# The order of an expert's last row groups, and of the second expert's transposes and w2 loads, in an attention + mixture-of-experts kernel

## The chip, the cores and the metric

The kernel runs on one core of one Trainium2 chip. The metric is device time in microseconds (us) of one execution, lower is better. In what follows PE is TensorE (matmuls; PEld its weight loads), DVE is VectorE, ACT is ScalarE, POOL is GpSimd and SP is SyncE, which here issues nearly all plain DMAs and all DMA transposes in one queue. POOL issues the indirect DMAs (gathers and scatters of rows).

## The reference, cut to what matters

Attention over 4 batches of 768 positions and 8 heads of 64 gives `x`, 3072 rows of 512. Then a mixture of experts is computed on `x`:

```python
logits = x @ w_gate
noisy_logits = logits + np.log1p(np.exp(x @ w_noise)) * noise
top2 = np.argpartition(-noisy_logits, 2, axis=1)[:, :2]   # two of eight experts for a row
...
for e in range(E):                                        # 8 experts
    for k in range(2):
        mask = top2[:, k] == e
        h = np.maximum(x[mask] @ w1[e], 0.0)               # 512 -> 1024
        out[mask] += top2_w[mask, k, None] * (h @ w2[e])   # 1024 -> 512
```

All of it is float32. The change touches the loop over the experts alone.

## The kernel before, in words

**Numbers.** TensorE works on float16. Each float32 operand is kept as a high half and a low half (names ending in `h` and `l`, such as `w1h`/`w1l`, `hth`/`htl`), and a product is three passes: high by high, low by high, high by low. ACT makes the high half by a cast, DVE the low half by a subtraction.

**Experts by rank.** The experts are sorted by how many rows chose them. Rank `e` has room for `CAPS[e]` rows: 800, 832, 808, 800, 784, 776, 768, 768. These are six groups of 128 rows (`c` = 0 to 5) and, up to rank 5, a last partial group (`c = LAST = 6`), the **tail**, of 32, 64, 40, 32, 16 and 8 rows. Where the tail has at most 32 rows (`four(e, c)`: ranks 0, 3, 4 and 5) its second matmul is spread over four quarters of the PE array, and DVE must add four quarters up (L920, four instructions) where a full group takes one (L931).

**Rows in.** For a group POOL gathers the rows into `xg` (L90), ACT and DVE make the halves in `x`, and SP issues a DMA transpose into `xte` (ranks 0 and 1: `x_gather`, `x_trans`, lines L812 to L814; later ranks `plan_x`: `xs_gather`, three DVE sums in `xs_sums` L1292 to L1296, `xs_hi` with L1312, `xs_lo` with L1322, transposes at L1328 into `xte`, `xl`, or borrowed parts of `w2h`/`w2l`).

**First matmul.** Ranks 0 and 1 use `mm1` (L854) in two column halves; rank 1's first half needs groups 0 to 2 transposed. From rank 2 on, `seven` computes it as seven products of half-sized blocks instead of eight (L1359). The products 1 and 5 of a rank's first slice form its **head** (`seven_head(n)`); the head reads the tail columns of `x` too. ACT copies their results (L1380, L1383), DVE adds them to later ones (L1385, L1387) and makes `htl` (L1394).

**Second matmul.** For each group, three passes of eight matmuls into one PSUM tile `pt` (two of these in turn): `w2h` by `hth`, `w2l` by `hth`, `w2h` by `htl` (L1431; the tail of quarters L1425; rank 0 L909). Then DVE scales the result and adds the earlier output `prev`, gathered by POOL, and POOL scatters `y` to `out`.

**Weights.** A quarter of w1 or w2 is 512 KB: `w_load` issues it on SP into one of four `stg` buffers, `w_hi` (ACT L740) and `w_lo` (DVE L758) split it. w1 of ranks 2 and later also gets sums (`plan_w1`: L1339, L1348, L1352).

**What sets the order.** Each engine runs its instructions in the order in which the program writes them. For ranks 1 and up, `on(t, f, ...)` files small steps under a number `t`, and `hook(t)` issues them; in the second matmul `hook(32 + 3c)`, `hook(33 + 3c)` and `hook(34 + 3c)` stand behind the first pass, the second pass and the output of group `c`. The groups run 0, 1, ..., 5, then the tail; the next rank's head stands ahead of the tail (or of group 5 where there is no tail). For rank 1 the code is written out: in rank 0's `mm1(0, 1, f)` loop, steps f = 2 to 5 split rank 1's w1 and load its w2, steps 5 to 7 transpose its groups 0 to 2; the loop over rank 0's groups 3 to 6 splits w2 and transposes groups 3 to 6.

Of the kernel before, what the change touches and what calls it, by code (L numbers as in the profile page):

```python
# [25 lines left out]
E, F = 8, 1024  # L26
# [37 lines left out]
def attn_moe(ctx, tc, qt, kt, vt, wgn, noise, w1, w2, out):  # L64
# [660 lines left out]
    def w_load(e, i):  # L725
        s = stage.tile([P, SW], F32, name="stg")[:, :1024]
        SG[e, i] = s
        if i == 0:
            EV[e] = nc.values_load(eid[0:1, e:e + 1], engines=[mybir.EngineType.SP], min_val=0, max_val=E - 1) if e else 0
        if i < 4:  # L730
            nc.sync.dma_start(s, w1.rearrange("e d f -> (e d) f")[bass.ds(EV[e] * DM + i * P, P)])
        else:
            i -= 4
            rows = bass.ds(EV[e] * F + 2 * i * P, 2 * P)
            nc.sync.dma_start(s.rearrange("p (c d) -> p c d", c=2),
                              w2.rearrange("e f d -> (e f) d")[rows].rearrange("(c p) d -> p c d", p=P))
# [51 lines left out]
    def chunks(e):  # L788
        return -(-CAPS[e] // P)
# [644 lines left out]
    for f in range(FC):  # L1434
        mm1(0, 1, f)
        if f < 2:
            gate_tr(f + 4, og)
        if f == 1:
            gate_ur(og)
            decode_rest()  # L1440
            last_ids()
        if 2 <= f < 6:
            w_split(1, f - 2)
            w_load(1, f + 2)
        if f == 5:
            count_over(og)
        if f > 1:
            x_gather(1, f - 2)
        if f > 4:
            x_trans(1, f - 5)  # L1450
    x_gather(1, 6)
    for c in range(3, chunks(0)):
        w_split(1, c + 1)
        x_trans(1, c)
        mm2(0, c, None)
    seven_init()
    G["w2"] = WT[0]
    for e in range(2, E):
# [28 lines left out]

    for e in range(1, E):
        pv = []

        def prev():
            if len(pv) < chunks(e):
                pv.append(prev_gather(e, len(pv)))

        n = e + 1
        if e == 1:
            on(0, tail_ids)
            plan_x(n, 0, 0, (3, 3, 3), (4, 4), (5, 5, 5, 5))
            plan_x(n, 1, 1, (6, 6, 6), (7, 7), (8, 8, 8, 8))
            plan_w1(n, 0, 1, 9, 9, 10, 10, 10)  # L1500
            plan_w1(n, 1, 2, 11, 11, 12, 12, 12)
            plan_x(n, 2, 7, (13, 13, 13), (14, 14), (15, 15, 15, 15))
            plan_w1(n, 2, 11, 33, 33, 34, 34, 34)
            plan_x(n, 3, 12, (35, 35, 35), (36, 36), (37, 37, 37, 37))
            plan_w1(n, 3, 13, 38, 38, 39, 39, 39)
        else:
            for i, (a, b) in enumerate(((3, 4), (4, 7), (8, 14), (15, 21))):
                on(a, w_hi, e, 4 + i)
                on(b, w_lo, e, 4 + i)
            on(36, tail_next, e)  # L1510
            if n < E:
                plan_x(n, 0, None, (9, 11, 12), (10, 13), (15, 16, 18, 19))
                plan_x(n, 1, None, (22, 23, 25), (24, 27), (28, 29, 29, 31))
                plan_w1(n, 0, 8, 32, 32, 33, 33, 34)
                plan_w1(n, 1, 15, 35, 35, 36, 36, 37)
                plan_x(n, 2, 20, (38, 38, 38), (39, 39), (40, 40, 40, 40))
                plan_w1(n, 2, 35, 41, 41, 42, 42, 43)
                plan_x(n, 3, 32, (44, 44, 44), (45, 45), (46, 46, 46, 46))
                plan_w1(n, 3, 38, 47, 47, 48, 48, 49)
            if e > 2:  # L1520
                on(4, w_load, e, 6)
                on(4, w_load, e, 7)
        if n + 1 < E:
            on(40 if e == 1 else 43, xs_gather, n + 1, 0)
            on(42 if e == 1 else 47, xs_gather, n + 1, 1)
        if n < E:
            on(44, w_load, n, 4)
            on(44, w_load, n, 5)
        if e == 1:
            on(48, w_load, n, 6)  # L1530
            on(48, w_load, n, 7)
        for t in (17, 20, 23):
            on(t, prev)
        if e == 1:
            for half in range(2):
                for f in range(FC):
                    mm1(e, half, f)
                    hook(8 * half + f)
            for t in range(16, 32):
                hook(t)  # L1540
        else:
            hi, lo = seven(e, 0, 2)
            hi()
            lo()
            hook(3)
            seven(e, 0, 6)
            for t in range(4, 7):
                hook(t)
            for i in range(1, 5):
                if i < 4:  # L1550
                    seven(e, i, 1)
                    hook(7 * i)
                    seven(e, i, 5)
                    hook(7 * i + 1)
                h7 = seven(e, i - 1, 7)
                h7[0]()
                hook(7 * i + 2 if i < 4 else 28)
                if i < 4:
                    h2 = seven(e, i, 2)
                    h2[0]()  # L1560
                    h7[1]()
                    hook(7 * i + 3)
                    seven(e, i, 6)
                    h2[1]()
                    hook(7 * i + 4)
                else:
                    py = psum.tile([P, 512], F32, name="pt", bufs=2)
                    mm2_part(e, 0, py, 0, range(7), True, False)
                    h7[1]()
                    hook(29)  # L1570
                h3 = seven(e, i - 1, 3)
                h3[0]()
                hook(7 * i + 5 if i < 4 else 30)
                h4 = seven(e, i - 1, 4)
                h4[0]()
                h3[1]()
                h4[1]()
                hook(7 * i + 6 if i < 4 else 31)
        for c in range(chunks(e)):
            if c == chunks(e) - 1 and n < E:  # L1580
                seven_head(n)
            if c or e == 1:
                py = psum.tile([P, 512], F32, name="pt", bufs=2)
                for i, k in enumerate((0, 2, 1)):
                    if e == 1:
                        mm2_pass(e, c, py, k, 1)
                    else:
                        mm2_part(e, c, py, k, range(FC), i == 0, i == 2)
                    if i < 2:
                        hook(32 + 3 * c + i)  # L1590
            else:
                for k in (2, 1):
                    mm2_part(e, 0, py, k, range(7), False, False)
                    hook(33 - k // 2)
                for k in (0, 2, 1):
                    mm2_part(e, 0, py, k, (7,), False, k == 1)
            mm2_out(e, c, py, pv[c])
            prev()
            hook(34 + 3 * c)
        for t in range(60):  # L1600
            hook(t)
# [104 lines left out]
```

## Time and profile before

| | us |
|---|---|
| three runs | 642.48, 644.54, 645.26 (median 644.54) |
| the profiled execution's own time | 642.6 |
| its span, first to last instruction | 640.8 |
| PE busy in the span | 622.5 |
| DVE busy | 481.3 |
| ACT busy | 315.9 |
| POOL busy | 249.0 |

The profiled execution is one run with its own time; the span is 1.8 us shorter. Attention and routing fill about the first 130 us, rank 0 lasts to about 201, rank 1 to about 268, and each later rank takes about 60. A row of the profile gives a line of the kernel, the engine, the operation, what it writes and reads, and its time; in square brackets stands how long the engine was idle before it, and what ended that.

### The profile page before, as it was taken

The page shows a single profiled execution, that of the slowest core. Times are in us where ns is not written, and L with a number is a line of the kernel's source. Part 1 is how long each engine was busy: PE and PEld are TensorE (multiplying, and loading weights), DVE is VectorE, ACT ScalarE, POOL GpSimd, SP SyncE. Part 2 cuts the span into 40 slices and gives each one's busy share as a digit, 9 for nine tenths or more (in the row PEclk, how much of TensorE's full clock was granted, in tenths as well). Part 3 has the DMA queues.
Part 4 walks back from the last instruction along what each step waited for, and adds up shares of the span by engine and source line. Part 5 has one row for each costly group of instructions (what it writes and reads, how often), then busy time and mean ns, then how long its engine had stood idle before and what let it go on. Part 6 is the DMA issues. An engine that isn't in the chain of part 4 may idle for free.

```text
span 640.8 us, 14153 instructions
## 1 busy us (share of the span) xinstructions
PE 622.5 (97%) x5295; PEld 358.8 (56%) x5295; DVE 481.3 (75%) x1039; ACT 315.9 (49%) x692; POOL 249.0 (39%) x432
## 2 busy tenths in 40 slices
PE   8999999999999999999999999999999999999995
PEld 7778777765654544555455544554554455445542
DVE  5768999889796797188868887987898679757410
ACT  4868988941253553075437534654464255425200
POOL 4442224203254324532573266336523532333041
PEclk9999999999999999999999999999999999999998
DMA  9999986788379976547886597759677767763021
GB/s 308 333 292 351 292 266 201 222 318 250 118 217 171 253 186 170 211 122 140 209 265 152 131 228 245 181 133 250 201 189 156 218 205 166 182 198 105 3 96 51
DMA packets 123708, 127.93 MB, mean 200 GB/s; under 512 B 83242, under 2 KB 86674, under 8 KB 123630
## 3 DMA queue, kind: packets, MB, share of 16 engines
q1 hardware_dynamic: 111838, 90.66, 53.3%
q0 software_dynamic: 11792, 36.27, 18.0%
q8 instruction: 44, 0.72, 0.5%
q14 instruction: 34, 0.28, 0.1%
HBM read 81.85 MB, written 25.61 MB: 168 GB/s over the span
## 4 chain that ended last, share of the span: by engine, by line
PE 82%; DVE 6%; issue 3%; DMA 3%; ACT 2%; POOL 1%; SPq 1%; POOLq 0%; DVEq 0%; ACTq 0%
PE pt L1431 29%; PE h L1359 16%; PE h L854 8%; PE pt L909 5%; PE pt L341 3%; PE pt L1359 3%; PE o L1359 3%; PE s L318 3%; PE o L354 3%; PE h L909 2%; DMA xte<-x 2%; PE pt L378 1%; PE o L246 1%; DVE y L920 1%; DVE htl L1394 1%
## 5 line engine op out<-in xcount | busy, mean ns | idle before, releaser
L90 POOL DMA_INDIRECT out_dram<-y,tb x52 | 69.3, 1333 | 169.4 <-DVE y L931 131.6
L90 POOL DMA_INDIRECT xg<-xd,tb x54 | 60.1, 1112 | 118.1 <-DVE dsc L653 32.3
L1431 PEld LDWEIGHTS <-hth 128*128 128x128 f16 x576 | 56.4, 98 | 66.7
L931 DVE SCALAR_TENSOR_TENSOR y<-pt,tb,prev 128x512 f32<-128x512 f32 x42 | 31.5, 750 | 67.4 <-PE pt L1431 49.8
L1359 PEld LDWEIGHTS <-w1h 128*128 128x128 f16 x504 | 48.9, 98 | 38.0 <-issue 4.1
L1431 PE MATMUL pt<-w2h,hth 128*128 128x512 f16 x288 | 69.0, 379 | 0.0
L1431 PE MATMUL pt<-w2h,htl 128*128 128x512 f16 x288 | 69.0, 379 | 0.0
L1431 PE MATMUL pt<-w2l,hth 128*128 128x512 f16 x288 | 69.0, 379 | 0.0
L1359 PEld LDWEIGHTS <-w1l 128*128 128x128 f16 x504 | 49.3, 98 | 34.9
L90 POOL DMA_INDIRECT prev<-out_dram,tb x45 | 52.4, 1165 | 23.7 <-issue 12.8
L333 ACT ACTIVATE p<-s,nm 128x120 f32<-128x120 f32 x192 | 51.0, 376 | 0.8
L854 PE MATMUL h<-xte,w1h 128*128 128x384 f16 (+2 forms) x248 | 48.9, 336 | 1.1 <-DMA xte<-x 1.1
L1431 PEld LDWEIGHTS <-htl 128*128 128x128 f16 x288 | 28.2, 98 | 34.0
L1348 ACT ACTIVATE w1h<-stg 128x768 f16<-128x768 f32 (+1 forms) x24 | 22.7, 944 | 37.9 <-DVE stg L1339 37.9
L1391 ACT ACTIVATE hth<-h 128x384 f16<-128x384 f32 (+4 forms) x48 | 23.8, 496 | 35.6 <-PE h L1359 35.6
L1348 ACT ACTIVATE w1l<-stg 128x768 f16<-128x768 f32 (+1 forms) x24 | 22.5, 942 | 37.2 <-DVE stg L1339 37.2
L1359 PE MATMUL h<-xte,w1h 128*128 128x384 f16 (+4 forms) x180 | 39.7, 329 | 0.7 <-DVE h L1385 0.4
L1359 PE MATMUL h<-xte,w1l 128*128 128x384 f16 (+4 forms) x180 | 39.7, 329 | 0.0
L1339 DVE TENSOR_TENSOR stg<-stg 128x256 f32<-128x256 f32 x96 | 36.2, 419 | 0.8
L854 PEld LDWEIGHTS <-w1h 128*128 128x128 f16 x256 | 24.7, 98 | 20.5 <-issue 2.2
L1312 ACT ACTIVATE x<-xt 128x512 f16<-128x512 f32 (+2 forms) x44 | 26.3, 625 | 19.6 <-issue 17.3
L1394 DVE SCALAR_TENSOR_TENSOR htl<-h,hth 128x384 f16<-128x384 f32 (+4 forms) x48 | 26.3, 562 | 11.8 <-ACT hth L1391 11.5
(301 smaller groups left out, 1292.0 us busy)
## 6 DMA issues: line engine op xcount, KB each, us to landing
stg<-in_w_dram SPq DMA_DIRECT2D x64, 512.0 KB
q<-in_qt_dram SPq DMA_DIRECT2D x24, 256.0 KB
xd<-x SPq DMA_DIRECT2D x24, 256.0 KB
out_dram<-xg SPq DMA_DIRECT2D x8, 768.0 KB
kb<-in_kt_dram SPq DMA_DIRECT2D x6, 768.0 KB
hth<-in_vt_dram SPq DMA_DIRECT2D x12, 260.0 KB
htl<-in_vt_dram SPq DMA_DIRECT2D x16, 195.0 KB
ve<-in_vt_dram SPq DMA_DIRECT2D x12, 260.0 KB
```

The costliest lines, as they stand in the source:

```text
L90: return nc.gpsimd.indirect_dma_start(**kw)
L333: nc.scalar.activation(PE_[t][:, a, hp, :], SC[t][:, a, hp, :], AF.Exp, bias=NM[t][:, 1, a, hp:hp + 1], scale=0.125)
L854: nc.tensor.matmul(ph[:, :n], w1_of(w, wn, c, f), x[:, xo + c, c0:c1], start=(k == 0), stop=(k == 11))
L909: nc.tensor.matmul(py, hx[:, f, c * P:c * P + P], wv[:, f, :], start=st, stop=sp)
L931: nc.vector.scalar_tensor_tensor(y, py[:, :d], gw, pv[:, :d], op0=OP.mult, op1=OP.add)
L1312: nc.scalar.activation(t[:r, c:c + k], src, AF.Copy)
L1339: nc.vector.tensor_tensor(o, x, y, op=op)
L1348: nc.scalar.activation(hi, x, AF.Copy, scale=W1S)
L1359: nc.tensor.matmul(ph[:, :h], w[:, la, a, P * j:P * j + P], x[:, j, :h], start=start and k == 0, stop=k == 5, skip_group_check=True)
L1391: nc.scalar.activation(hh[:, f, t], src, AF.Relu)
L1394: nc.vector.scalar_tensor_tensor(hl[:, f, t], src, 0.0, hh[:, f, t], op0=OP.max, op1=OP.subtract)
L1431: nc.tensor.matmul(py, x, wv[:, f, :], start=st, stop=sp, skip_group_check=True)
```

## The change

The diff does two things.

- **Second rank (e = 1).** In rank 0's last stretch the transposes of rank 1's groups 0 to 3 move into steps f = 4 to 7 of the `mm1` loop, its w2 loads go behind them (two at f = 6 and 7, two in the loop over rank 0's groups), two of the four w1 splits move into that loop, and the w2 splits move behind it; the last three go to the first three hooks of rank 1's own `mm1`. The sums and splits of rank 2's first groups are filed two hooks later. `count_over` goes behind the loop.
- **Tails (ranks 3, 4 and 5).** The tail is computed ahead of group 5 (`early`, `turns`), and the next rank's head is put behind group 5's second pass. The steps of the next rank's tail are filed one hook earlier, those of its last w1 quarter under the new places.

```diff
-        if 2 <= f < 6:
+        if 2 <= f < 4:
             w_split(1, f - 2)
-            w_load(1, f + 2)
-        if f == 5:
-            count_over(og)
+        if f > 3:
+            x_trans(1, f - 4)
         if f > 1:
             x_gather(1, f - 2)
-        if f > 4:
-            x_trans(1, f - 5)
+        if f > 5:
+            w_load(1, f - 2)
     x_gather(1, 6)
+    count_over(og)
     for c in range(3, chunks(0)):
-        w_split(1, c + 1)
-        x_trans(1, c)
+        if c < 5:
+            w_split(1, c - 1)
+            w_load(1, c + 3)
+        if c < 6:
+            x_trans(1, c + 1)
         mm2(0, c, None)
+    w_split(1, 4)
...
+        turns = list(range(chunks(e)))
+        early = e > 1 and chunks(e) > LAST and four(e, LAST)
+        if early:
+            turns[-2:] = turns[:-3:-1]
...
-            plan_x(n, 0, 0, (3, 3, 3), (4, 4), (5, 5, 5, 5))
-            plan_x(n, 1, 1, (6, 6, 6), (7, 7), (8, 8, 8, 8))
+            for t, i in ((0, 5), (1, 6), (2, 7)):
+                on(t, w_split, n - 1, i)
+            plan_x(n, 0, 0, (5, 5, 5), (6, 6), (7, 7, 7, 7))
+            plan_x(n, 1, 1, (8, 8, 8), (9, 9), (10, 10, 10, 10))
...
-                plan_x(n, 3, 32, (44, 44, 44), (45, 45), (46, 46, 46, 46))
-                plan_w1(n, 3, 38, 47, 47, 48, 48, 49)
+                plan_x(n, 3, 32, *(((43, 43, 43), (44, 44), (45,) * 4) if early else ((44, 44, 44), (45, 45), (46,) * 4)))
+                plan_w1(n, 3, 38, *((50, 50, 51, 47, 48) if early else (47, 47, 48, 48, 49)))
...
-        for c in range(chunks(e)):
-            if c == chunks(e) - 1 and n < E:
+        for m, c in enumerate(turns):
+            if c == turns[-1] and n < E and not early:
                 seven_head(n)
...
                     if i < 2:
                         hook(32 + 3 * c + i)
+                    if i == 1 and early and c == turns[-1]:
+                        seven_head(n)
...
-            mm2_out(e, c, py, pv[c])
+            mm2_out(e, c, py, pv[m])
```

**Place 1, SP, rank 0's last stretch.** The queue before: w2 loads of rank 1 (`stg<-in_w2`), then the transposes of its groups.

```order
L735 DMA stg_3536<-in_w2_dram 128x2x512
...
L735 DMA stg_3605<-in_w2_dram 128x2x512
L814 DMA_TRANSPOSE xte_2960<-x_3622 128x8x128
L814 DMA_TRANSPOSE xte_2960<-x_3645 128x8x128
L814 DMA_TRANSPOSE xte_2960<-x_3668 128x8x128
L814 DMA_TRANSPOSE xte_2960<-x_3678 128x8x128
```

The same queue with the change:

```order
L814 DMA_TRANSPOSE xte_2960<-x_3576 128x8x128
L814 DMA_TRANSPOSE xte_2960<-x_3599 128x8x128
L814 DMA_TRANSPOSE xte_2960<-x_3622 128x8x128
...
L735 DMA stg_3630<-in_w2_dram 128x2x512
L814 DMA_TRANSPOSE xte_2960<-x_3647 128x8x128
...
L735 DMA stg_3655<-in_w2_dram 128x2x512
```

Three transposes now stand ahead of the first w2 load, where four loads stood ahead of the first transpose.

**Place 1, ACT, the same stretch.** L860 is rank 0's relu of slice f, L740 the cast of a weight quarter, L812 the cast of a gathered group; before, from the relu of f = 4:

```order
L860 ACTIVATE hth_89<-h_3565 128x416
L740 ACTIVATE w1h1_2956<-stg_3308 128x1024
L860 ACTIVATE hth_89<-h_3588 128x416
L740 ACTIVATE w1h1_2956<-stg_3310 128x1024
L812 ACTIVATE x_3622<-xg0_165 128x512
L860 ACTIVATE hth_89<-h_3626 128x416
L812 ACTIVATE x_3645<-xg0_165 128x512
L860 ACTIVATE hth_89<-h_3649 128x416
```

With the change, from the same relu:

```order
L860 ACTIVATE hth_89<-h_3561 128x416
L812 ACTIVATE x_3576<-xg0_165 128x512
L860 ACTIVATE hth_89<-h_3584 128x416
L812 ACTIVATE x_3599<-xg0_165 128x512
L860 ACTIVATE hth_89<-h_3607 128x416
L812 ACTIVATE x_3622<-xg1_166 128x512
L860 ACTIVATE hth_89<-h_3632 128x416
L812 ACTIVATE x_3647<-xg1_166 128x512
```

Three casts of gathered groups now stand ahead of the last relu (f = 7), where two stood.

**Place 2, SP, the end of rank 3.** The transposes of 16 columns are those of rank 4's tail: two of high halves, then two of low halves (into `xl`). Before:

```order
L735 DMA stg_5750<-in_w2_dram 128x2x512
...
L735 DMA stg_5752<-in_w2_dram 128x2x512
L1328 DMA_TRANSPOSE xte_2629<-x_5762 128x6x16
L1328 DMA_TRANSPOSE xte_2629<-x_5766 128x8x16
L1328 DMA_TRANSPOSE xl_2961<-x_5784 128x6x16
L1328 DMA_TRANSPOSE xl_2961<-x_5788 128x8x16
```

With the change:

```order
L1328 DMA_TRANSPOSE xte_2629<-x_5750 128x6x16
L1328 DMA_TRANSPOSE xte_2629<-x_5754 128x8x16
...
L735 DMA stg_5758<-in_w2_dram 128x2x512
...
L735 DMA stg_5760<-in_w2_dram 128x2x512
L1328 DMA_TRANSPOSE xl_2961<-x_5770 128x6x16
L1328 DMA_TRANSPOSE xl_2961<-x_5774 128x8x16
```

The two w2 loads moved from ahead of the high halves to between the high and the low halves.

**Place 2, DVE, the end of rank 3.** L1322 makes the low halves of rank 4's tail, the L931 of `prev_2964` is the output of group 4, L920 those of the tail. Before:

```order
L931 SCALAR_TENSOR_TENSOR y<-pt,tb,prev_2964 128x512
L1322 TENSOR_TENSOR x<-xg_166,x 16x512
L1322 TENSOR_TENSOR x<-xg_166,x 16x256
L1322 TENSOR_TENSOR x<-xt,x 16x512 x2
L1339 TENSOR_TENSOR stg<-stg 128x256 x4
L1352 SCALAR_TENSOR_TENSOR w1l_2957<-stg,w1l_2957 128x768
L931 SCALAR_TENSOR_TENSOR y<-pt,tb,prev_2965 128x512
L1352 SCALAR_TENSOR_TENSOR w1l_2957<-stg,w1l_2957 128x1024
L920 SCALAR_TENSOR_TENSOR y<-pt,tb,prev_2966 32x512
L920 SCALAR_TENSOR_TENSOR y<-pt,tb,y 32x512 x3
L1394 SCALAR_TENSOR_TENSOR htl<-o,hth 128x392
L1385 TENSOR_TENSOR h<-h,p_5853 128x392
```

With the change:

```order
L1322 TENSOR_TENSOR x<-xg_166,x 16x512
L1322 TENSOR_TENSOR x<-xg_166,x 16x256
L1322 TENSOR_TENSOR x<-xt,x 16x512 x2
L931 SCALAR_TENSOR_TENSOR y<-pt,tb,prev_2964 128x512
L1339 TENSOR_TENSOR stg<-stg 128x256 x4
L920 SCALAR_TENSOR_TENSOR y<-pt,tb,prev_2965 32x512
L920 SCALAR_TENSOR_TENSOR y<-pt,tb,y 32x512 x3
L1352 SCALAR_TENSOR_TENSOR w1l_2957<-stg,w1l_2957 128x768
L1352 SCALAR_TENSOR_TENSOR w1l_2957<-stg,w1l_2957 128x1024
L931 SCALAR_TENSOR_TENSOR y<-pt,tb,prev_2966 128x512
L1394 SCALAR_TENSOR_TENSOR htl<-o,hth 128x392
L1385 TENSOR_TENSOR h<-h,p_5873 128x392
```

The low halves moved ahead of group 4's output, and the tail's four additions moved from just ahead of rank 4's first L1394 and L1385 to ahead of two w1 splits and group 5's output.

## Rows read from the trace of the kernel before

**Rows 1.** The page, busy time: us, share of the span and instructions of each engine.

```profile
PE 622.5 (97%) x5295; PEld 358.8 (56%) x5295; DVE 481.3 (75%) x1039; ACT 315.9 (49%) x692; POOL 249.0 (39%) x432
```

**Rows 2.** Busy time by stretch. The columns are the stretch, its length, then busy us (and instructions) of PE, PEld, DVE, ACT and POOL, the granted clock of PE, the DMA engines' mean busy share, and GB/s.

```profile
200.90:202.10 1.20, 0.11 (x5) 0.08 (x2) 1.20 (x3) 0.00 (x0) 1.20 (x1) 1.00 1.03 211
202.10:633.00 430.90, 429.81 (x2377) 222.40 (x2378) 315.01 (x542) 185.27 (x320) 177.92 (x286) 1.00 0.67 175
394.00:407.00 13.00, 12.71 (x91) 6.86 (x90) 11.17 (x19) 8.49 (x16) 3.45 (x6) 1.00 0.66 198
455.00:468.00 13.00, 12.64 (x92) 6.91 (x90) 11.19 (x19) 8.48 (x17) 4.07 (x6) 1.00 0.66 198
516.00:529.00 13.00, 12.57 (x93) 6.91 (x90) 11.22 (x19) 8.62 (x16) 3.33 (x6) 1.00 0.63 198
```

**Rows 3.** The chain of work that ended last, two pieces ahead of rank 1's first matmul: start, length, what.

```profile
186.74 3.94 DMA xg<-xd,tb
190.68 11.24 DMA xte<-x
```

**Rows 4.** The timeline of SP's queue in that stretch: start, length of the issuing, line, what, count.

```profile
179.39 5.27 SPq L735 DMA_DIRECT2D stg<-in_w_dram  x4
186.61 18.39 SPq L814 DMA_TRANSPOSE xte<-x  x7
```

**Rows 5.** The timeline of the engines in that stretch, cut to the gathers of rank 1's groups 2 and 4 (POOL), the casts of its groups 1, 2, 4 and 5 (ACT L812), rank 0's relu of f = 7 (ACT L860), and the first matmuls of rank 0's groups 3 and 5 and of rank 1 (PE).

```profile
180.56 1.31 POOL L90 DMA_INDIRECT xg<-xd,tb  x1 [0.23 <-issue]
183.85 1.89 PE L909 MATMUL pt<-w2h,hth 128*128 128x512 f16 x8
184.17 0.63 ACT L812 ACTIVATE x<-xg 128x512 f16<-128x512 f32 x1 [1.72 <-DMA xg<-xd,tb]
184.71 0.50 ACT L860 ACTIVATE hth<-h 128x416 f16<-128x416 f32 x1
...
186.73 0.63 ACT L812 ACTIVATE x<-xg 128x512 f16<-128x512 f32 x1 [1.52 <-DMA xg<-xd,tb]
186.74 1.00 POOL L90 DMA_INDIRECT xg<-xd,tb  x1 [3.15 <-DVE x L813]
...
194.21 1.89 PE L909 MATMUL pt<-w2h,hth 128*128 128x512 f16 x8
...
195.55 0.63 ACT L812 ACTIVATE x<-xg 128x512 f16<-128x512 f32 x1 [4.34 <-issue]
...
202.05 0.81 PE L854 MATMUL h<-xte,w1h 128*128 128x384 f16 x4 [1.09 <-DMA xte<-x]
```

**Rows 6.** The timeline of a gather with few other transfers about it, and of the cast that waited for it (rank 0's group 3).

```profile
147.97 1.00 POOL L90 DMA_INDIRECT xg<-xd,tb  x1 [19.83 <-DVE dsc L653]
...
151.99 0.63 ACT L812 ACTIVATE x<-xg 128x512 f16<-128x512 f32 x1 [2.90 <-DMA xg<-xd,tb]
```

**Rows 7.** The groups of instructions by line, the split of a w2 quarter on DVE (count, busy us, mean ns, idle before).

```profile
L758 DVE SCALAR_TENSOR_TENSOR w2l<-stg,w2h 128x1024 f16<-128x1024 f32 x28 | 33.5, 1215 | 0.0
```

**Rows 8.** The busy time of the stretch of rank 1's first matmul, and of the 2.4 us in which the two w2 loads at the end of rank 3 moved, by the columns of rows 2.

```profile
200.00:236.00 36.00, 34.91 (x213) 19.16 (x206) 28.77 (x51) 17.14 (x32) 14.94 (x26) 1.00 0.90 220
384.70:387.10 2.40, 2.40 (x12) 1.07 (x11) 0.76 (x2) 1.98 (x3) 1.96 (x5) 1.00 1.02 351
```

**Rows 9.** The timeline at the end of rank 3, up to the head of rank 4: SP's w2 loads and the transposes of rank 4's tail, ACT's last cast for them, DVE's output of group 4 and low halves, PE's first two passes of group 5 and the head, whose matmuls on `xl` read the low halves.

```profile
381.71 1.17 SPq L735 DMA_DIRECT2D stg<-in_w_dram  x2
383.25 4.05 SPq L1328 DMA_TRANSPOSE xte<-x  x2
...
385.53 0.63 ACT L1312 ACTIVATE x<-xt 16x512 f16<-16x512 f32 x1 [0.21 <-DVE xt L1296]
...
387.11 1.89 PE L1431 MATMUL pt<-w2h,hth 128*128 128x512 f16 x8
387.31 0.75 DVE L931 SCALAR_TENSOR_TENSOR y<-pt,tb,prev 128x512 f32<-128x512 f32 x1 [1.82 <-PE pt L1431]
...
388.84 1.89 PE L1431 MATMUL pt<-w2l,hth 128*128 128x512 f16 x8
...
389.03 2.37 SPq L1328 DMA_TRANSPOSE xl<-x  x2
...
392.29 0.83 PE L1359 MATMUL o<-xte,w1h 128*128 128x392 f16 x4
392.96 0.49 PE L1359 MATMUL o<-xl,w1h 128*128 128x392 f16 x2
...
393.95 0.49 PE L1359 MATMUL h<-xl,w1h 128*128 128x392 f16 x2
```

**Rows 10.** The timeline behind that: rank 3's tail on PE, its four additions on DVE, rank 4's products after its head, and the add (L1385) that one of them waits for.

```profile
394.38 0.61 PE L1425 MATMUL pt<-w2h,hth 128*32 128x512 f16 x8
395.79 0.84 PE L1359 MATMUL o<-xte,w1h 128*128 128x392 f16 x4
395.91 0.74 DVE L920 SCALAR_TENSOR_TENSOR y<-pt,tb,prev 32x512 f32<-32x512 f32 x1 [1.53 <-PE pt L1425]
396.68 2.31 DVE L920 SCALAR_TENSOR_TENSOR y<-pt,tb,y 32x512 f32<-32x512 f32 x3
...
399.50 0.56 DVE L1385 TENSOR_TENSOR h<-h,p 128x392 f32<-128x392 f32 x1
...
400.12 0.82 PE L1359 MATMUL h<-xte,w1h 128*128 128x392 f16 x4 [0.18 <-DVE h L1385]
```

More of the change, by code (lines that the diff above doesn't have):

```diff
@@ L1489, in attn_moe @@
         pv = []
+        turns = list(range(chunks(e)))
+        early = e > 1 and chunks(e) > LAST and four(e, LAST)
+        if early:
+            turns[-2:] = turns[:-3:-1]
         def prev():
             if len(pv) < chunks(e):
-                pv.append(prev_gather(e, len(pv)))
+                pv.append(prev_gather(e, turns[len(pv)]))
         n = e + 1
```

## The prediction

> **What bounds the kernel now.** I read the page first: PE is busy 97% of the span, far above any other engine [rows 1]. So I looked for the stretches in which PE is not busy. From 202.1 to 633 it is busy 429.81 of 430.90 us, and the missing 1.09 us lie in three short stretches, one behind each tail of quarters: 0.29, 0.36 and 0.43 us [rows 2]. Just ahead, between 200.9 and 202.1, it is idle for 1.09 us, ended by the landing of a transpose into `xte` [rows 2, 5]. These are the places that the diff touches, and together they are 2.18 us of 642.6 us, the profiled execution's own time. That is the first thing to see: nothing in the diff removes PE work, so what it can win in the expert loop is bounded by 2.18 us, or 0.34%.
>
> The first wait, read backwards through the chain: rank 1's first matmul waits for a transpose that SP issued at 190.68 and that landed 11.24 us later [rows 3]. SP issued its four w2 loads from 179.39 on and the seven transposes behind them [rows 4]. The other three waits are alike; at the end of rank 3, DVE spends 395.91 to 398.99 on the four additions of the tail, gets to the add L1385 only at 399.50, and PE waits 0.18 us for it, with a smaller wait behind it [rows 2, 10].
>
> **The change, second rank.** It moves instructions; it adds and removes none. The profiled execution is the base: 642.6 us.
>
> *The wait at 201.* Groups 0 to 2 are gathered at the same time as before, since these gathers stand ahead of everything moved. In place of two casts there are now three ahead of the last relu on ACT, and the first transposes have no load ahead of them in SP's queue. Before, the third landed 11.24 us after its issue [rows 3]; the third cast can be done when the gather of group 2 has landed, at the latest 186.73 as now [rows 5], plus 0.63 for the cast and as much for DVE, so even with 11.24 us again the transposes are in at about 199.3, ahead of 200.96. Term: -1.09 us. What would be late next for rank 1's first matmul is w1's last split; it now stands behind group 3's output, which is due by 194.21 [rows 5], and so has over five us to spare.
>
> *The last relu.* It is now behind the cast of group 2 (before: of group 1). PE's first pass of rank 0's group 3 starts at 183.85 and comes to its eighth matmul 7/8 of 1.73 us later, at 185.36; that one needs the relu [rows 5]. From the landing of the gather the relu is done in 1.1 us (184.17 to 185.21). The gather of group 2 is issued at 180.56. With 4.0 us, as the quiet gather took [rows 6], it lands at 184.6 and PE waits 0.3 us; landing at 186.73 as it did before, beside the loads, PE waits 2.5 us. A faster landing costs nothing, and a gain is excluded, since PE did not wait here. Now no load runs beside it, so I take a value near the quiet row: 0.1 us.
>
> *Group 3's output.* On DVE it is now behind group 4's low half (before: group 3's). PE needs its PSUM tile again at 194.21 for group 5 [rows 5]. From the landing of the gather to the end of that output are 0.63 + 0.69 + 0.75, so 2.1 us, by the cast, a half of the same size and an output of a full group [rows 5, 9]. The gather can be issued at about 183.6 (before 186.74) and took 8.8 us (186.74 to 195.55) beside loads and transposes, 4.0 us in quiet [rows 5, 6]: landing 187.6 to 192.4, output done by 189.7 to 194.5. Cost 0 to 0.3 us; I take 0.1.
>
> Here a rule bears. The seven transposes kept SP issuing for 18.39 us [rows 4]. The Trainium skill (Advanced Engine Details and Errata, section X-Bar Transpose (TRN2)) says that a transpose DMA is as fast as a plain one, 350 to 400 GB/s. By that three transposes of 256 KB would be gone in about 2.2 us, an estimate from that page, gather 4 would meet nearly nothing, and this term would be 0. The trace disagrees: six such transposes and a half one, 1.7 MB, took 18.39 us to be handed over, about 90 GB/s [rows 4].
>
> *w2 splits.* Three more splits of 1.215 us on DVE [rows 7] fall into rank 1's first matmul, where DVE is busy 28.77 of 36 us [rows 8]: 3.6 us into 7.2 us free, none of it ahead of a matmul that is due. w2 is needed at 236, 25 us later. Cost 0; without that cover it would be PSUM banks coming free late, at most 1.2 us a slice.
>
> Sum of the second rank: -1.09 + 0.1 + 0.1 = -0.9 us.
>
> **The change, tails.** Worked out at the end of rank 3; rank 4 is built alike, rank 5 has no next tail.
>
> *The waits behind the tail.* The four additions (3.08 us, 0.74 + 2.31) now run during group 5's passes; ahead of L1394 and L1385 DVE has one output of 0.75 us [rows 9, 10]. The inputs of these two come only when PE has done two more products of 1.0 us (395.79 on), so DVE is free when they come. Term: -0.29, -0.36 and -0.43 [rows 2], -1.08 together.
>
> *PSUM at the tail.* Low halves now stand ahead of group 4's output on DVE, in the 1.82 us for which it idled [rows 9]. The last needs ACT's cast, done at 386.16, so DVE is through at about 387.8 and the output at 388.5; PE's tail ends at 387.11 + 1.41 = 388.52 [rows 9, 10] and group 5 takes that PSUM tile. 0 to 0.1 us, taken as 0.
>
> *The head's low halves.* The head now starts at 388.52 + 2 x 1.73 = 391.98, 0.31 us earlier than 392.29, and reads low halves 0.67 and 1.66 us later [rows 9], at 392.65 and 393.64. Their transposes were issued at 389.03 and about 390.2, in a queue that held nothing more than high halves. Now the two w2 loads stand directly ahead of them: SP can issue the loads only after the second high-half transpose, whose cast is done at 386.16, so from about 387.3 to 388.5, and the low halves at 388.5 and 389.7. The loads are 1.05 MB; at the 351 GB/s at which they moved [rows 8] that is 3.0 us. If that time is all over by then, nothing waits: 0. If all of it is added to the 3.9 us that sufficed before (389.03 to 392.96), the first low half is there at 395.4 and PE waits 2.75 us. If the loads move from the middle of their hand-over on, they end at about 391.3; the two small transposes, 2.37 us of issuing for both [rows 9], then bring the first at about 392.5 to 393, a wait of 0 to 0.4. I take 0.4 us, nearer the lower end, at each of the two boundaries (ranks 3 and 4): +0.8 us.
>
> Sum of the tails: -1.08 + 0.8 = -0.3 us. Both parts: -1.2 us, so 641.4 us for an execution like the profiled one. That one lies 1.9 us under the median of the runs, 644.54; on the median the forecast is 643.3 us.
>
> **The rivals.**
>
> *Everything goes and nothing comes late:* -2.2 us, 642.3. For it: PE is idle in just these places, and DMA has slack behind each. Against: two reads have less than half a microsecond of room.
>
> *The head waits for the low halves behind the loads*, the case that ends slower. Place: PE's first matmul on `xl` at the ends of ranks 3 and 4. Price: up to 2.75 us each. It decides from about 1.0 us each, where (0.9 + 1.08) / 2 is used up. With 1.7 us each the sum is -0.9 - 1.08 + 3.4 = +1.4, 645.9 us; with 2.75 it is +3.5, 648.0. For it: what stands ahead in SP's queue delays what is behind, as the 11.24 us of the transpose behind loads and transposes show [rows 3, 4]. Against: the loads then had larger transposes ahead of them, which now are gone by the time they are issued.
>
> *The last relu waits for the gather of group 2 as long as it lands today:* +2.4 us over the forecast, 645.7. For it: ACT stops in order at that cast. Against: the loads that slowed the gather are no longer there.
>
> *The order does not bring the transposes in earlier*, because they are slow beside the gathers whichever way they are queued: the 1.09 us stay, 644.4. Against: there are more than ten us of room.
>
> **How the numbers follow.** Chances: forecast 0.50, all goes 0.22, head waits 0.12, relu waits 0.11, no earlier transposes 0.05. The range has to hold the first two, most of the next two, and the spread of three runs, 642.48 to 645.26, which is larger than any term here: 641.2 to 646.2 us. A difference of under 0.5%, 3.2 us, cannot be told from no change in a measurement of this kernel. Faster by more would need more than all the idle time of PE in the places touched: 0.03. Slower by more needs the head's wait near its upper end, or two of the rivals at once: 0.07. Within: 0.90.
>
> **What would show it.** In the changed profile PE's idle time ahead of rank 1's first matmul should be gone, and the waits for L1385 and L1394 behind the tails too. Right or wrong for the costs: an idle PE at the eighth matmul of rank 0's group 3 (relu), ahead of group 5 (PSUM), or ahead of the first matmul on `xl` in a head (low halves). The forecast is wrong if PE's idle time in the expert loop falls by all of 2.2 us or grows, or if the time moves by over 3 us without PE's idle time.

## The result, and the profile after

The changed kernel is slower by 0.93%, which is outside the predicted range:

| | median, us | lowest to highest, us | runs |
|---|---|---|---|
| before | 644.77 | 642.48 to 649.47 | 9 |
| after | 650.09 | 646.81 to 653.57 | 9 |

The ratio is 1.0093, with a 95% interval of 1.0068 to 1.0118. The profiled execution of after took 653.57 us (span 651.8).

Busy time by stretch, by the columns of [rows 2]: the stretch around rank 1's first matmul, the ends of ranks 3 and 4 with the stretch between them, and the rest.

```profile
203.20:204.40 1.20, 1.20 (x25) 0.45 (x18) 0.55 (x1) 0.00 (x0) 0.38 (x1) 1.00 1.14 354
...
394.00:403.00 9.00, 4.44 (x18) 1.96 (x17) 2.98 (x4) 0.98 (x2) 4.82 (x6) 0.83 1.02 290
403.00:461.00 58.00, 58.00 (x323) 29.53 (x322) 49.46 (x87) 29.31 (x50) 25.91 (x40) 1.00 0.73 161
461.00:468.00 7.00, 4.49 (x17) 1.98 (x16) 2.85 (x4) 0.97 (x2) 4.81 (x6) 0.78 0.99 318
468.00:644.00 176.00, 176.00 (x953) 91.28 (x952) 116.38 (x196) 70.28 (x122) 60.54 (x94) 1.00 0.58 147
```

What PE waited for from 135 us on: engine, line, releaser, us in total, times, longest.

```profile
PE o L1359 <- DMA xl<-x: 4.6, 1, 4.6
PE o L1359 <- DMA xte<-x: 2.5, 1, 2.5
```

All the idle time of [rows 2] is gone: the 1.09 us ahead of rank 1's first matmul, and the waits behind the three tails, of which the last, at the end of rank 5, lies in the last stretch, where PE is busy for the whole 176 us. In their place stand just two waits, of 4.56 and 2.51 us, in two stretches of 9 and 7 us. The second thing to see is the column behind POOL: the granted clock in these two stretches is 0.83 and 0.78 of full speed, and 1.00 in the other stretches.

The timeline of the end of rank 3, answering [rows 9 and 5]; first PE at rank 1's first matmul, then SP, DVE's low halves, and PE from the head on.

```profile
204.30 0.82 PE L854 MATMUL h<-xte,w1h 128*128 128x384 f16 x4
...
385.51 4.05 SPq L1328 DMA_TRANSPOSE xte<-x  x2
...
388.62 1.27 DVE L1322 TENSOR_TENSOR x<-xt,x 16x512 f16<-16x512 f32 x2
...
389.76 1.07 SPq L735 DMA_DIRECT2D stg<-in_w_dram  x2
390.93 2.92 SPq L1328 DMA_TRANSPOSE xl<-x  x2
...
394.34 0.83 PE L1359 MATMUL o<-xte,w1h 128*128 128x392 f16 x4
399.73 0.56 PE L1359 MATMUL o<-xl,w1h 128*128 128x392 f16 x2 [4.56 <-DMA xl<-x]
400.09 1.51 PE L1359 MATMUL h<-xte,w1h 128*128 128x392 f16 x4
401.40 0.86 PE L1359 MATMUL h<-xl,w1h 128*128 128x392 f16 x2
402.05 2.58 PE L1431 MATMUL pt<-w2h,htl 128*128 128x512 f16 x8
404.46 0.83 PE L1359 MATMUL o<-xte,w1h 128*128 128x392 f16 x4
```

And the chain of work that ended last, at the ends of ranks 3 and 4 (start, length, what), with one piece of six matmuls between.

```profile
390.93 8.77 DMA xl<-x
...
404.63 0.99 PE o L1359 x6
...
457.79 6.70 DMA xte<-x
```

On SP the two w2 loads (389.76) now stand between the tail's high halves (385.51) and its low halves (390.93). The first low half, a transpose of 16 rows, lands 8.77 us after its issue at the end of rank 3 and 6.70 us at the end of rank 4; in the kernel before 3.9 us sufficed. The head's four matmuls on the high halves run at 394.34, and its fifth, the first on `xl`, waits until 399.73. Then the matmuls are slow: four of 392 columns take 1.51 us where they took 0.83, eight of 512 columns 2.58 where they took 1.89 [rows 9]. The trace has the granted clock at 0.5 (1.2 GHz of 2.4) from 400.02 to 403.44 and from 464.88 to 468.29, 3.41 us each, right behind the two waits. At half clock 3.41 us do the work of 1.71, so each fall costs 1.7 us more.

### The profile page after: what moved, and what is told of

It reads as the page before. It is cut to its first block, busy times and chain, and to the rows that moved or that the text cites. A ratio compares the mean times of both kernels' runs of the same rounds, so it can differ in the third digit from the quotient of the medians.

```text
span 651.8 us, 14157 instructions
## 1 busy us (share of the span) xinstructions
PE 626.6 (96%) x5295; PEld 361.0 (55%) x5295; DVE 482.1 (74%) x1039; ACT 315.4 (48%) x692; POOL 254.7 (39%) x432
## 4 chain that ended last, share of the span: by engine, by line
PE 85%; DVE 8%; DMA 3%; ACT 2%; issue 2%; POOL 0%; POOLq 0%; DVEq 0%
PE pt L1431 25%; PE h L1359 19%; PE h L854 10%; PE pt L909 7%; PE pt L1359 4%; PE o L1359 4%; PE pt L341 3%; PE o L354 3%; PE s L318 3%; PE h L909 2%; PE o L246 1%; DMA xl<-x 1%; DVE x L1322 1%; PE pt L378 1%; DVE nm L325 1%
## 5 line engine op out<-in xcount | busy, mean ns | idle before, releaser
L90 POOL DMA_INDIRECT out_dram<-y,tb x52 | 72.7, 1399 | 167.1 <-DVE y L931 136.8
L931 DVE SCALAR_TENSOR_TENSOR y<-pt,tb,prev 128x512 f32<-128x512 f32 x42 | 31.4, 748 | 74.5 <-PE pt L1431 58.7
L1431 PE MATMUL pt<-w2h,htl 128*128 128x512 f16 x288 | 70.5, 385 | 0.0
L1394 DVE SCALAR_TENSOR_TENSOR htl<-h,hth 128x384 f16<-128x384 f32 (+4 forms) x48 | 26.6, 563 | 12.4 <-ACT hth L1391 12.1
```

What stands on the lines that cost most here:

```text
L90: return nc.gpsimd.indirect_dma_start(**kw)
L931: nc.vector.scalar_tensor_tensor(y, py[:, :d], gw, pv[:, :d], op0=OP.mult, op1=OP.add)
L1394: nc.vector.scalar_tensor_tensor(hl[:, f, t], src, 0.0, hh[:, f, t], op0=OP.max, op1=OP.subtract)
L1431: nc.tensor.matmul(py, x, wv[:, f, :], start=st, stop=sp, skip_group_check=True)
```

## The experiments

Three theories. **Queue:** the loss is the head's wait for the low halves behind the two loads on SP, and the half clock that follows. **Head too early:** the low halves are late for the new head wherever the loads are. **Elsewhere:** the second rank, or the attention stage, which took 3.4 us longer in the first profile of after than in that of before. Besides the medians, a stretch that no attention stage enters is compared: from rank 0's first matmul on `xte` and `w1h` to the end of PE's last matmul, called the expert stretch below. It is 503.2 us in the first profile of before and 510.8 in that of after.

### Each half alone

The tails back as they were:

```
-        early = e > 1 and chunks(e) > LAST and four(e, LAST)
+        early = False
```

> Second-rank part alone; the tails are back in their old place. Queue theory (the loss is the head's wait for the tail's low-half transposes, which stand behind two w2 loads in SP's queue, and the half clock after it): nothing of the loss is here, the wait of 1.09 us at rank 1's first matmul is gone, 643.4 to 644.1 beside 644.8 of the kernel before, PE without a gap over 0.5 us after 134 us and its clock at 1.00 to the end. Rival (the second-rank part or the attention stage, which took 3.4 us longer in the profiled run, carries the loss): 648 or more.

643.11 us, just under the expected range, ratio 0.9999 (0.9980 to 1.0017): no loss here, and no gain either. PE's waits from 135 us on:

```profile
PE pt L909 <- ACT hth L860: 0.9, 1, 0.9
PE h L1359 <- DVE h L1385: 0.6, 3, 0.2
PE h L1359 <- DVE htl L1394: 0.2, 1, 0.2
```

The wait at rank 1's first matmul is gone, but a wait of 0.92 us for the last relu of rank 0 (L860) is there, which the same code did not have in the full change and the expectation did not have either. The waits of the tails (L1385, L1394) are back, and the clock stays at 1.00.

The other half: the second rank's code as in the kernel before, the tails changed (its hunk ahead of the tails is undone, of which the core is):

```
-        if 2 <= f < 4:
+        if 2 <= f < 6:
             w_split(1, f - 2)
-        if f > 3:
-            x_trans(1, f - 4)
+            w_load(1, f + 2)
...
+        if f > 4:
+            x_trans(1, f - 5)
```

> Tails part alone; the second rank is back as it was before. Queue theory: the whole loss is here, 650 to 652 (the changed kernel's 650.1 and the 1.1 us that the second rank no longer gives back), with the two waits in the chain on transposes into xl and xte and a clock of 0.5 behind each. Rival (the second-rank part carries it): 644 to 645.

651.22 us, ratio 1.0131 (1.0111 to 1.0150), with waits of 2.32 us for `xl` and 2.60 us for `xte`, and 3.41 us at clock 0.5 at the end of each. The whole loss lies in the tails. But rank 1's first matmul did not wait at all, though the order there is that of the kernel before. So that kernel was profiled again:

> The kernel before, unchanged, profiled once more, since the second-rank part alone gained nothing and the tails alone showed no wait at rank 1's first matmul though its order there is that of the kernel before. If that wait is a matter of the execution (when the last rank 0 and rank 1 transfers land), it is shorter than 0.5 us or gone here, and rank 1 starts right behind the last matmul of rank 0. If it belongs to the code: 1.0 to 1.2 us again.

641.04 us, and these waits of PE from 135 us on:

```profile
PE h L1359 <- DVE h L1385: 0.6, 3, 0.2
PE h L1359 <- DVE htl L1394: 0.2, 1, 0.2
```

No wait for a transpose: the 1.09 us of [rows 2, 5] belong to that one execution. The expert stretch is 502.1 us here, 1.1 shorter than in the first profile.

### Moving the loads

The loads behind the low halves:

```
-            on(44, w_load, n, 4)
-            on(44, w_load, n, 5)
+            on(46 if early else 44, w_load, n, 4)
+            on(46 if early else 44, w_load, n, 5)
```

> The whole change, with the next rank's w2 loads 4 and 5 filed one hook later (46 for 44) at the ends of ranks 3, 4 and 5, so that on SP they stand behind the tail's low-half transposes. Queue theory: the transposes land in some 3 us as the high halves do, no wait before the head, the clock stays, and all terms of the gain show: 642.0 to 643.2. Rival (the head stands too early for the transposes wherever the loads are: DVE's low halves and the transposes themselves are late): waits of 1 us or more stay, 647 to 650.

642.12 us, ratio 0.9983 (0.9958 to 1.0007). PE has no wait of over 0.02 us from 135 us on, and the clock stays. The end of rank 3, SP and the head:

```profile
387.06 2.45 SPq L1328 DMA_TRANSPOSE xl<-x  x2
389.71 5.12 SPq L735 DMA_DIRECT2D stg<-in_w_dram  x4
...
391.75 0.83 PE L1359 MATMUL o<-xte,w1h 128*128 128x392 f16 x4
392.41 0.49 PE L1359 MATMUL o<-xl,w1h 128*128 128x392 f16 x2
```

The head stands as early as in the full change, behind the second pass, and reads the low halves 5.4 us after their issue without waiting. That refutes "too early". The loads ahead of the high halves, at hook 44 but registered first, so that they keep their old place in the queue:

```
+                if early:
+                    on(44, w_load, n, 4)
+                    on(44, w_load, n, 5)
...
-            on(44, w_load, n, 4)
-            on(44, w_load, n, 5)
+            if not early:
+                on(44, w_load, n, 4)
+                on(44, w_load, n, 5)
```

> The whole change, with the same two loads ahead of the tail's high-half transposes, where they stood before, at the ends of ranks 3, 4 and 5. Queue theory in its narrow form (what costs is that the loads are fresh when the low halves are issued): the loads start some 5 us before the low halves and are mostly landed, the waits fall under 1 us each, 642.3 to 644. In its wide form (any load still running delays the transposes): waits of 1 to 3 us stay, 645 to 649. Rival (the head is too early wherever the loads are): 647 to 650, as in the run with the loads last.

642.65 us, ratio 0.9982 (0.9968 to 0.9995), again with no wait. SP at the end of rank 3:

```profile
381.78 1.09 SPq L735 DMA_DIRECT2D stg<-in_w_dram  x2
383.28 4.05 SPq L1328 DMA_TRANSPOSE xte<-x  x2
387.43 2.44 SPq L1328 DMA_TRANSPOSE xl<-x  x2
```

Loads issued 5.65 us ahead of the low halves do no harm; loads issued 1.2 us ahead of them do. By its interval this kernel is faster than the one before, if only by 0.2%. The expert stretch is 500.0 us in both kernels of this section, 2.0 less than in the second profile of before.

Then the reverse, the fault alone in the kernel before:

```
-            on(44, w_load, n, 4)
-            on(44, w_load, n, 5)
+            on(45 if 2 < e < 6 else 44, w_load, n, 4)
+            on(45 if 2 < e < 6 else 44, w_load, n, 5)
```

> The kernel before, with nothing of the change but this: the two w2 loads are filed one hook later at the ends of ranks 3, 4 and 5 (45 for 44), so that they stand between the tail's high-half and low-half transposes on SP. Queue theory: the wait appears in the kernel before as well. The low halves are then issued at some 390 and land 6.5 to 8.8 us later, while the head wants them at 393: waits of 3 to 6 us at the ends of ranks 3 and 4, each with a clock of 0.5 for 3.4 us behind it (1.7 us), 652 to 658. Rival (it takes the new order of the tails or the early head as well): no wait, 643 to 646.

652.6 us, ratio 1.0114 (1.0087 to 1.0141).

```profile
389.62 1.07 SPq L735 DMA_DIRECT2D stg<-in_w_dram  x2
391.15 2.38 SPq L1328 DMA_TRANSPOSE xl<-x  x2
...
394.42 0.83 PE L1359 MATMUL o<-xte,w1h 128*128 128x392 f16 x4
397.69 0.49 PE L1359 MATMUL o<-xl,w1h 128*128 128x392 f16 x2 [2.44 <-DMA xl<-x]
398.02 0.92 PE L1359 MATMUL h<-xte,w1h 128*128 128x392 f16 x4
```

With its old head and its old order of tails the kernel before gets the same wait (2.44 us, under the expected 3, and 3.50 at the end of rank 4) and 3.41 us at clock 0.5 about the end of each. The order of a few instructions on SP is sufficient for the whole loss.

### The length of the wait, and the clock

The head one pass later:

```
-                    if i == 1 and early and c == turns[-1]:
+                    if i == 2 and early and c == turns[-1]:
```

> The whole change with the loads where it put them, but the head one pass later, behind group 5's third pass and ahead of its output. Queue theory: the transposes land when they did, so each wait shrinks by the pass that now runs ahead of it, 1.73 us: 4.56 to about 2.8 and 2.51 to about 0.8 by the changed kernel's profile, 2.32 and 2.60 to 0.6 and 0.9 by the profile of the tails alone. If only a long idle time halves the clock, one or both of the clock's falls go too: 644 to 647. Rival (the low halves come later when the head comes later, since SP or DVE is what is late): the waits stay at 2.3 to 4.6 us, 649 to 651.

644.83 us, ratio 1.0006 (0.9981 to 1.0031). The waits are 0.71 and 0.78 us. Busy time at the ends of ranks 3 and 4:

```profile
390.00:404.00 14.00, 13.29 (x84) 6.79 (x77) 10.84 (x17) 5.90 (x9) 8.46 (x13) 1.00 0.89 284
...
456.00:470.00 14.00, 13.22 (x80) 7.57 (x79) 10.48 (x17) 8.23 (x15) 7.03 (x10) 1.00 0.82 258
```

The wait shrinks by the pass that now covers it, and the clock stays at 1.00.

Idle time filled with work that changes nothing:

```
+    FILL = {4: 26, 5: 14}
...
             x = xs_of(e, lb, b)
+            if lb and start and a == 0 and b == 0 and f == 0:
+                for i in range(FILL.get(e, 0)):
+                    nc.tensor.matmul(G["b5"][0][:, :h], G["wp"][0][:, 0, 0, :P], xs_of(e, 0, 0)[:, i % 2, :h], start=True,
+                                     stop=True, skip_group_check=True)
```

> The changed kernel with idle time filled: ahead of the head's first low-half matmul stand 26 further matmuls at the end of rank 3 and 14 at the end of rank 4 (128 x 392, 0.166 us each, so 4.3 and 2.3 us), on the high halves into a bank that the head overwrites next. The transposes are as late as before. If the clock falls because TensorE stood idle: no idle time over some 0.5 us, clock 1.00 to the end, and the two times 1.7 us of half clock are saved: 646 to 647.5 beside 650.1 of the changed kernel (a little more where the transposes land early and the fill is too long). Rival (the clock falls for another reason, or its fall cost nothing because work behind it was waiting anyway): 649.5 to 651.

650.66 us, so the expected 646 to 647.5 was missed. The profile has one wait left, of 0.58 us, and the clock did stay:

```profile
390.00:404.00 14.00, 14.00 (x93) 7.07 (x92) 8.31 (x14) 2.22 (x4) 8.58 (x12) 1.00 0.85 271
456.00:470.00 14.00, 13.42 (x86) 6.91 (x79) 8.84 (x15) 3.98 (x6) 8.44 (x13) 1.00 0.85 268
```

The expert stretch is 507.5 us, 3.3 less than in the first profile of after, as two falls of 1.7 us would give. Yet I had sized the fill by the longest wait seen, and it costs its 6.6 us in every execution. Two more runs, side by side, answer that: the unchanged after, and the fill cut to `{4: 14, 5: 14}`.

> The changed kernel, unchanged, with a second profile. From its first profile and the one of the tails alone, the wait of the two boundaries together is 7.1 and 4.9 us, so that it varies from execution to execution. Queue theory: two waits on low-half transposes again, between 2 and 5 us each, each followed by 3.4 us at a clock of 0.5, and no other idle time over 0.5 us in the experts' stage but perhaps one at the last relu of rank 0; 649 to 651.5. Rival (the first profile was an outlier and the usual loss lies elsewhere): waits under 1 us in this profile at a time near 650.

> The changed kernel with 14 further matmuls (2.3 us) ahead of the head's first low-half matmul at both boundaries, where the filled run had 26 and 14: the longer fill cost 4.3 us in every execution, also in those whose transposes land after 2.3. If the clock falls because of the idle time, the fill leaves at most some 2 us of it at rank 3 and little at rank 4, at least one of the two falls goes, and in executions with short waits both: 646 to 649, below the changed kernel of the same call by 1.7 to 3.4 us. Rival (the fall of the clock costs the time nothing): within 1 us of the changed kernel of the same call, or above it.

After again: 652.0 us, a little above the expected range, ratio 1.0111 (1.0071 to 1.0151). Filled with 14: 648.91 us, ratio 1.0063 (1.0040 to 1.0086), so 3.1 us less with 28 matmuls more. The two intervals overlap, but the profiles show the same difference: the expert stretch is 511.1 us in after again and 508.0 with the fill. In the latter's profile the waits left are 1.01 and 1.04 us, and the clock stays at 1.00 to PE's end. The waits of after in its second profile:

```profile
PE o L1359 <- DMA xte<-x: 3.4, 1, 3.4
PE o L1359 <- DMA xl<-x: 2.9, 1, 2.9
PE pt L909 <- DVE y L929: 1.1, 1, 1.1
```

Together the head's waits are 6.3 us here, 7.1 in the first profile, 4.9 in the tails alone: their length varies by execution, their place does not. The third row is the prediction's term for group 3's output: group 5 of rank 0 waits 1.12 us for its PSUM tile, which the expectation for this run did not have.

### Why the loads were slow

The gather of x for the rank after next goes out on POOL beside the two loads. Here it stands behind the tail's output:

```
-            on(40 if e == 1 else 43, xs_gather, n + 1, 0)
+            on(40 if e == 1 else 52 if early else 43, xs_gather, n + 1, 0)
```

> The changed kernel with its loads where the change put them, but the gather of x for group 0 of the rank after next, whose two halves go out on POOL at 388.98 and 390.50 beside the two loads, filed behind the tail's output instead, at the ends of ranks 3 and 4 (and 5, where none is left). It tells why the loads took 8.3 us where the prediction gave them 3.0. If they share the DMA engines with these gathers: without them the low halves land 1.5 us or more earlier, the waits fall from 2.3 to 4.6 us to 0 to 2.5, 645 to 649. If the loads and the transposes are this slow by themselves: waits of 2.3 to 4.6 us as before, 649.5 to 652.

646.11 us, ratio 1.0026 (0.9999 to 1.0053), with waits of 1.31 and 1.41 us and the clock at 1.00. The DMA view of 388 to 400 us, 40 slices of 0.3 us, and the two kinds of queue (packets, MB, share); first the changed kernel:

```profile
GB/s 382 123 27 0 109 123 164 362 185 48 82 89 171 266 328 355 382 389 382 396 382 253 201 224 236 232 201 152 87 34 27 34 19 444 219 423 342 389 239 416
...
q0 software_dynamic: 373, 1.20, 45.2%
q1 hardware_dynamic: 848, 1.47, 38.9%
```

and with the gather later:

```profile
GB/s 0 0 191 382 300 27 0 0 218 96 307 287 103 68 61 212 382 389 362 355 389 362 341 413 364 403 229 115 68 14 7 0 0 102 109 212 328 389 416 335
...
q1 hardware_dynamic: 1006, 1.71, 46.3%
q0 software_dynamic: 240, 0.79, 18.7%
```

and its timeline:

```profile
390.80 1.07 SPq L735 DMA_DIRECT2D stg<-in_w_dram  x2
391.97 2.88 SPq L1328 DMA_TRANSPOSE xl<-x  x2
...
397.52 0.49 PE L1359 MATMUL o<-xl,w1h 128*128 128x392 f16 x2 [1.31 <-DMA xl<-x]
```

Without the gather the traffic behind the issue at 390.80 starts to run at full rate at 392.8 only, then moves 341 to 413 GB/s for ten slices, 3.0 us. That is 1.13 MB, most of it the 1.05 MB of the two loads. By the trace's completion signals the loads are complete at 395.04 and 396.62, the second 5.8 us after the first issue, and the first low half at 397.48. So the prediction's 3.0 us for moving the loads was about right, but some 2 us ahead of them and 0.8 us behind them were missing; what fills the 2 us no run shows. With the gather beside them, 0.4 MB more of the software queue moves in the same 12 us, and the loads are complete at 395.88 and 398.09, 8.3 us after the first issue.

### The second rank's worth

The tails of after with the loads behind the low halves (the edit 46 for 44 above), and the second rank as in the kernel before (the hunk above undone):

> The tails part with the two loads behind the low halves, and the second rank as it was in the kernel before; beside the run of the whole change with the loads last (642.1) it gives the worth of the second-rank part by itself. If the wait at rank 1's first matmul is a matter of the execution, and the second-rank part trades it for one at the last relu of rank 0 as often: 641.5 to 643, no difference that can be measured. If the second-rank part is worth its 1.1 us in most executions: 643 to 643.5.

643.03 us, ratio 0.9982 (0.9951 to 1.0012), and an expert stretch of 500.0 us, as with the second rank's part. The median lies on the border of the two expected ranges, but ratio (0.9983 with the part, 0.9982 without) and stretch are the same: no difference can be measured.

## Why the prediction was wrong

**The step that failed is the head's low halves**: 0.4 us at each of two boundaries, with bounds of 0 to 2.75. Measured were 4.56 and 2.51, then 2.92 and 3.40, and with the tails alone 2.32 and 2.60: three of the six above the bound, and none near 0.4. The issue times were forecast rightly: after's expert loop runs 2.25 us later at rank 1's first matmul (204.30 against 202.05), and 390.93 less that is 388.7, where 388.5 was forecast. What came after was not. The loads were taken to move from the middle of their hand-over at the 351 GB/s of [rows 8], and to be gone 3.0 us later. They came to full rate only 2 us after their issue even without the gather, and beside it they were complete 8.3 us after their issue. That row was a stretch in which they were already moving, so it held no start. The kernel before had the number: its two loads, handed over from 381.71 on [rows 9], are complete at 387.13 and 388.48 by its trace, 6.8 us after the first issue. From the forecast hand-over at 387.3 that is 394.1; with the 0.9 and 1.6 us by which the first low half landed behind the loads in the two profiles compared above, an estimate of the wait is 2.3 to 3.1 us. (By the prediction's own rule the loads would move from 387.9, the middle of a hand-over from 387.3 to 388.5, and end at 390.9, not at its 391.3; that slip made the term larger, not smaller.) The upper bound failed for the same reason: it was again those 3.0 us, added to a transpose time that had held without loads in front.

**The clock was not in the sum.** The first profile of before showed 1.00 at every place read, beside idle stretches of at most 1.09 us, and waits were priced at their own length. Each of the two waits brought 1.7 us more. Both together close the account of the first profile against the second one of before: 7.1 us of waits, 3.4 of half clock and 0.3 for two stops of the pipeline (below), less 2.0 recovered, are +8.8 us; the expert stretch grew by 8.7.

**The slower rival was the right mechanism**, with its place and sign, at 12 in 100. Its price ended at 648.0 us, as it took the same upper bound and no clock. Its argument "against", that the larger transposes ahead of the loads would be gone by then, was true and beside the point: the loads did it.

**The waits behind the tails** went, and PSUM at the tail cost nothing, both as forecast, but they were worth 2.0 us and not 1.08. The sum of PE's idle gaps is 1.09 in the second profile of before. Each gap also costs the time in which the pipeline runs empty. In the groups by line of after:

```profile
L1359 PE MATMUL o<-xte,w1h 128*128 128x392 f16 x16 | 3.3, 329 | 0.0
```

One matmul stands with 329 ns, yet six in a row take 0.99 us of the chain, 0.165 each; the rest, 0.16 us, overlaps with the next matmul unless that one waits. Six waits give 1.0 us, and 1.09 + 1.0 = 2.1. No run tried this by itself, but it fits every profile: 500.0 us (the three without a wait), plus PE's idle time, 0.16 us for each wait, 1.7 for each fall of the clock and 0.165 for each matmul of a fill, is within 0.25 us of the expert stretch in 13 of the 14 profiles. In the other, the loads between in the kernel before, it is 0.5 us too long; there the clock began to fall 0.6 us ahead of the end of a wait. The bound of 2.18 us on what the change could win was thus too low as well: from 503.2 to 500.0 us are 3.2.

**The wait at 201**, -1.09 us, was in the one profile I read. Of the five profiles with the second rank's old order (before twice, the tails alone, the tails with the loads last, the loads between) one has it. What the new order risks was priced at 0.1 us each: the last relu waited in one of nine profiles with the new order (0.92 us), and group 3's output in three (0.52, 0.56 and 1.12 us), above the bound of 0.3. A mean of 0.2 us goes and 0.35 come, so the term is about nothing, as the half alone and the last run above show. By the rule on transposes that was weighed there (the Trainium skill, Advanced Engine Details and Errata, X-Bar Transpose (TRN2)) the output's wait should have been 0; six of nine profiles agree and three don't. The 90 GB/s that the prediction set against it is a rate of hand-over beside gathers. Where the transposes had the DMA engines nearly to themselves, from 201.4 to 202.6 us in the first profile of before, these moved 280 GB/s. The rival that the relu waits was thus half right: it happens, seldom. The w2 splits cost nothing, as forecast: no profile has a wait for them.

## What to carry to other kernels

A hook or a list of callbacks is an order for every queue that its entries issue on: moving one entry to another hook can put a large load in front of a small transfer that is needed soon, on a queue that the change does not name. Compare the order on SP for each boundary, and price a transfer that is queued behind a fresh load by start, move and sharing together, from a like load's issue to its completion in the trace, not by the load's rate. And one profiled execution does not say whether a wait of 1 us that ends with a DMA is there in most executions: profile the kernel before twice ahead of counting on it.

## What was not expected of the hardware

- In the expert stretch PE's granted clock fell to 0.5 for 3.41 us within 1 us of the end of each of the eight long waits (2.32, 2.44, 2.51, 2.60, 2.92, 3.40, 3.50 and 4.56 us), and stayed at 1.00 about the twelve waits of 0.52 to 1.41 us. With matmuls in the idle time it did not fall, and 28 matmuls of work for nothing made the changed kernel 3.1 us faster (648.91 beside 652.0).
- Two 512 KB loads moved mostly within 3.0 us but were complete only 5.8 us after their first issue, and 8.3 us after it with gathers beside them; the transposes of 16 rows behind them landed 0.9 and 1.6 us after the loads.
- With the same code ahead of it, rank 0's first matmul started at 130.0 to 134.9 us in these profiles. That spread is larger than most terms here, so single profiles were compared from there on.
